# One casting queue for all loads, statistics batched by two pairs, and the last store moved: a small post-norm kernel

## The chip, the cores and the metric

The kernel runs on one core of a Trainium2 chip. The metric is the device time of one execution in microseconds (us). Each comparison runs both kernels in rounds on the same chip. A run counts as slow here when it lies over 1.5% above the fastest of the same kernel, for one core has no second die to be compared with.

Profiles name the engines PE (TensorE; PEld is its loading of weights), ACT (ScalarE), DVE (VectorE), POOL (GpSimd) and SP (SyncE, which here only issues transfers); a q at the end is the engine's instruction queue. SBUF is the memory that the engines work in, PSUM the one that TensorE writes to. A transfer is in flight from its issue until it lands, that is until its last part has arrived.

## The reference

```python
# x: (4, 256, 256), w_block: (256, 256), gamma: (256,), all float32
h = np.maximum(x @ w_block, 0.0)
y = x + h
mu = y.mean(-1, keepdims=True)
sigma = np.sqrt(y.var(-1, keepdims=True) + 1e-6)
return ((y - mu) / sigma * gamma).astype(np.float32)
```

## The kernel before

The 1024 rows are eight tiles of 128 rows, worked in four pairs ("waves", here x0 to x3). For a pair: transpose on TensorE, copy to SBUF on ACT, multiply by the weights on TensorE, relu on ACT, add x and take statistics on DVE; then, two pairs later in the program, square root on ACT, reciprocal and scale on DVE, normalise (one tile on DVE, one on ACT), multiply by gamma, store. The first pair and the weights come over SP's queue in fp32, the rest over GpSimd's, which casts to bf16 on the way.

```python
psum_t16 = tc.tile_pool(name="psum_t16", bufs=2, space=PSUM)
ident16, ident32 = ...                              # made on GpSimd
nc.sync.dma_start(x32_head, x_v[:, 0:WAVE, :])      # first pair, fp32, SP
nc.sync.dma_start(w32, w_block.rearrange("(c p) n -> p c n", p=P))
for wv in range(1, n_waves):                        # casting DMAs, GpSimd
    nc.gpsimd.dma_start(x16_rest[:, lo:lo+WAVE, :], x_v[:, wv*WAVE:(wv+1)*WAVE, :])
nc.gpsimd.dma_start(gamma_bc, gamma[None, :].to_broadcast((P, D)))
for c in range(KC):
    nc.vector.tensor_copy(w_sb[:, c], w32[:, c])
nc.scalar.activation(warm, warm, AF.Square)
# ... phase_a(w): transposes, copy xT, products psH, relu y_w, add x ...
for j in range(WAVE):
    nc.vector.bn_stats(bn6[:, j], y_w[:, j])
    nc.vector.bn_aggr(mv[:, j], bn6[:, j])
# ... phase_b(w) ...
nc.scalar.activation(sig, mv[:, :, 1], AF.Sqrt, bias=eps_sb)
nc.vector.reciprocal(rstd, sig)
nc.vector.scalar_tensor_tensor(out=nmr, in0=mv[:, :, 0], scalar=-1.0, ...)
# ... two normalisations into o1, then the multiply by gamma ...
if last:  # fp32, SP
    nc.vector.tensor_mul(of32_last, o1, gamma...); nc.sync.dma_start(dst, of32_last)
else:     # bf16, cast by the store
    nc.vector.tensor_mul(of16_all[...], o1, gamma...); nc.gpsimd.dma_start(dst, of16_all[...])
```

The order in which each engine runs its instructions is not the order of this text: the framework schedules them when the kernel is built.

## Time and profile before

| | |
|---|---|
| time, median of 6 runs | 24.76 us (24.53 to 25.16) |
| span of the profiled run | 23.0 us |
| first transpose starts / first relu starts | 4.54 / 7.37 us |
| last relu ends | 14.51 us |
| last multiply ends / last store lands | 19.05 / 22.1 us |

A timeline line gives start, duration (both us), engine, source line, operation, written and read tiles, shapes, count; in brackets stands how long the engine had been idle and what released it. These are two groups of products of the same shape and number, from the timeline of the kernel before:

```profile
6.30 1.04 PE L113 MATMUL psH<-w_sb,xT 128*128 128x256 bf16 x4 [0.68 <-ACT xT L108]
...
13.26 0.61 PE L113 MATMUL psH<-w_sb,xT 128*128 128x256 bf16 x4 [2.46 <-ACT xT L108]
```

The first four products take 1.04 us, the last four 0.61: TensorE runs slowly until late in the kernel. And this is the first of GpSimd's work after the start-up, in the place that the prediction gives to the first load:

```profile
0.74 0.20 POOL masks.py:197 MEMSET ident_82<- 128x128 bf16 x1 [0.29 <-POOLq L204]
```

### The profile page before, as it was taken

What the parts mean: (1) busy time and instruction counts of PE and PEld (TensorE: products, weight loads), DVE (VectorE), ACT (ScalarE), POOL (GpSimd) and SP (SyncE); (2) the same over time, 40 slices, a digit from 0 to 9 for tenths busy, and PEclk for the clock granted to TensorE, in tenths of its full rate; (3) what the DMA queues carried; (4) which work ended last, traced back from release to release, by engine and by line L of the source; (5) the groups of instructions that cost most, each with busy time, mean ns of one, the idle gap of its engine ahead of it and who ended that gap; (6) DMA issues with size and microseconds to landing.
All of it is one profiled execution on the core that took longest, in us unless ns stands there. A gap on an engine that the chain in (4) does not pass through costs nothing.

```text
span 23.0 us, 195 instructions
## 1 busy us (share of the span) xinstructions
PE 5.9 (26%) x32; PEld 4.0 (17%) x32; DVE 9.5 (42%) x40; ACT 10.2 (44%) x19; POOL 4.9 (21%) x15
## 2 busy tenths in 40 slices
PE   0000000197099949998000091000000000000000
PEld 0000000190078726763000050000000000000000
DVE  0100000016000099829970794699999891000000
ACT  0698000001801995376999937940696900000000
POOL 3699998000000000000000000005301762000000
PEclk9999999999999999999999997555555555555555
DMA  0003569999992000000000000000087029997000
GB/s 0 0 0 136 152 203 301 244 162 123 194 156 36 4 0 0 0 0 0 0 0 0 0 0 0 0 0 0 0 264 193 0 86 371 303 357 246 7 0 0
DMA packets 1568, 2.03 MB, mean 88 GB/s; under 512 B 160, under 2 KB 928, under 8 KB 1568
## 3 DMA queue, kind: packets, MB, share of 16 engines
q0 software_dynamic: 1008, 1.25, 25.9%
q1 hardware_dynamic: 560, 0.79, 10.6%
HBM read 1.44 MB, written 1.05 MB: 108 GB/s over the span
## 4 chain that ended last, share of the span: by engine, by line
ACT 21%; PE 21%; DMA 16%; DVE 12%; issue 5%; POOLq 2%; POOL 2%
DMA x_head<-in_x_dram 16%; PE psH L113 16%; ACT y_w L122 8%; ACT xT L108 7%; ACT L140 6%; PE psT L105 5%; DVE of_all L176 3%; DVE bn_201 L133 3%; POOLq L215 2%; POOL out_dram L181 2%; DVE nmr L144 2%; DVE rstd L142 1%; ACT sig L140 1%; DVE o_224 L151 1%; DVE o_213 L151 1%
## 5 line engine op out<-in xcount | busy, mean ns | idle before, releaser
L181 POOL DMA_DIRECT2D out_dram<-of_all x3 | 1.6, 536 | 13.6 <-DVE of_all L176 12.2
L113 PE MATMUL psH<-w_sb,xT 128*128 128x256 bf16 x16 | 3.6, 382 | 3.5 <-ACT xT L108 3.5
L122 ACT ACTIVATE y_w<-psH 128x512 bf16<-128x512 f32 x4 | 2.4, 597 | 2.6 <-PE psH L113 2.6
L113 PEld LDWEIGHTS <-xT 128*128 128x128 bf16 x16 | 1.7, 128 | 4.8 <-ACT xT L108 4.4
L105 PE MATMUL psT<-ident_87,x_head 128*128 128x128 f32 x4 | 1.1, 428 | 4.5 <-DMA x_head<-in_x_dram 4.5
L79 DVE CAST w_sb<-w_94 128x256 bf16<-128x256 f32 x2 | 0.5, 290 | 4.2 <-DMA w_94<-in_w_block_dram 4.2
L108 ACT CAST xT<-psT 128x512 bf16<-128x512 f32 x1 | 0.6, 585 | 3.4 <-PE psT L105 3.4
L105 PE MATMUL psT<-ident_82,x_rest 128*128 128x128 bf16 x12 | 1.9, 313 | 0.0
L70 POOL DMA_DIRECT2D x_rest<-in_x_dram x3 | 1.7, 587 | 0.0
L124 DVE TENSOR_TENSOR y_w<-y_w,x_head 128x512 bf16<-128x512 bf16 x1 | 0.7, 693 | 2.4 <-ACT y_w L122 2.4
L126 DVE TENSOR_TENSOR y_w<-y_w,x_rest 128x512 bf16<-128x512 bf16 x3 | 1.2, 415 | 1.0 <-ACT y_w L122 1.0
L108 ACT COPY xT<-psT 128x512 bf16<-128x512 bf16 x3 | 1.6, 584 | 0.0
L85 ACT ACT_TABLE_LOAD x1 | 1.3, 1283 | 0.7 <-PEq L204 0.7
L105 PEld LDWEIGHTS <-x_rest 128*128 128x128 bf16 x12 | 1.5, 151 | 0.3
L105 PEld LDWEIGHTS psT<-ident_87,x_head 128*128 128x128 f32 x4 | 0.7, 217 | 4.5 <-issue 4.5
L140 ACT ACT_TABLE_LOAD x1 | 1.3, 1283 | 0.0
L140 ACT ACTIVATE sig<-mv,eps_sb 128x2 f32<-128x2 f32 x4 | 1.2, 288 | 0.0
L160 ACT ACTIVATE o_213<-y_w,nmr,rstd 128x256 bf16<-128x256 bf16 x1 | 0.6, 600 | 1.1 <-DVE nmr L144 1.1
L142 DVE RECIPROCAL rstd<-sig 128x2 f32<-128x2 f32 x4 | 0.6, 160 | 0.9 <-ACT sig L140 0.9
L133 DVE BATCH_NORM_STATS2 bn_127<-y_w 128x6 f32<-128x256 bf16 x2 | 0.8, 418 | 0.0
L133 DVE BATCH_NORM_STATS2 bn_148<-y_w 128x6 f32<-128x256 bf16 x2 | 0.8, 418 | 0.0
L133 DVE BATCH_NORM_STATS2 bn_201<-y_w 128x6 f32<-128x256 bf16 x2 | 0.7, 414 | 0.0
(29 smaller groups left out, 9.8 us busy)
## 6 DMA issues: line engine op xcount, KB each, us to landing
out_dram<-of_all POOLq DMA_DIRECT2D x3, 256.0 KB, 2.8
x_rest<-in_x_dram POOLq DMA_DIRECT2D x3, 128.0 KB, 4.7
x_head<-in_x_dram SPq DMA_DIRECT2D x1, 256.0 KB, 3.7
w_94<-in_w_block_dram SPq DMA_DIRECT2D x1, 256.0 KB, 3.9
out_dram<-of_last SPq DMA_DIRECT2D x1, 256.0 KB, 3.0
gamma_bc<-in_gamma_dram POOLq DMA_DIRECT2D x1, 64.0 KB, 4.7
```

Of the source, the lines that this page charges most:

```text
L70: nc.gpsimd.dma_start(x16_rest[:, lo : lo + WAVE, :], x_v[:, wv * WAVE : (wv + 1) * WAVE, :])
L85: nc.scalar.activation(warm, warm, AF.Square)
L105: nc.tensor.transpose(psT[:, j, c, :], x_of(w, j)[:, ts(c, P)], idt)
L108: nc.scalar.copy(xT, psT)
L113: nc.tensor.matmul(psH[:, j, :], lhsT=xT[:, j, c, :], rhs=w_sb[:, c, :], start=(c == 0), stop=(c == KC - 1),)
L122: nc.scalar.activation(y_w, psH, AF.Relu)
L124: nc.vector.tensor_add(y_w, y_w, x32_head)
L126: nc.vector.tensor_add(y_w, y_w, x16_rest[:, (w - 1) * WAVE : w * WAVE, :])
L133: nc.vector.bn_stats(bn6[:, j], y_w[:, j])
L140: nc.scalar.activation(sig, mv[:, :, 1], AF.Sqrt, bias=eps_sb)
L142: nc.vector.reciprocal(rstd, sig)
L181: nc.gpsimd.dma_start(dst, of16_all[:, lo : lo + WAVE, :])
```

## The change

The intent was to drop the weight casts and the fp32 transposes, to keep SP out, and to halve the number of small statistics operations. The diffs in this document are shortened: dots, and lines in words, stand for code left out.

```diff
-    stats = ...bufs=n_waves + 2        psum_t16 = ...bufs=2
+    stats = ...bufs=4                  psum_t16 = ...bufs=3
+    w_sb = const.tile([P, KC, D], BF16)
+    nc.gpsimd.dma_start(w_sb, w_block.rearrange("(c p) n -> p c n", p=P))
+    x16_all = xin.tile([P, n_tiles, D], BF16)
+    nc.gpsimd.dma_start(x16_all[:, 0:WAVE, :], x_v[:, 0:WAVE, :])
     ident16 = ...
-    ident32, x32_head and w32 on SP, x16_rest
+    for wv in range(1, n_waves):
+        nc.gpsimd.dma_start(x16_all[:, lo:lo+WAVE, :], x_v[:, lo:lo+WAVE, :])
-    for c in range(KC): nc.vector.tensor_copy(w_sb[:, c], w32[:, c])
...
-            nc.vector.bn_aggr(mv[:, j], bn6[:, j])
+            nc.vector.bn_aggr(mv_all[:, w * WAVE + j], bn6[:, j])
-    sqrt, reciprocal, nmr per pair
+    def run_chain(w):                 # once for two pairs
+        nc.scalar.activation(sig_all[:, sl], mv_all[:, sl, 1], AF.Sqrt, bias=eps_sb)
+        nc.vector.reciprocal(rstd_all[:, sl], sig_all[:, sl])
+        nc.vector.scalar_tensor_tensor(out=nmr_all[:, sl], ...)
...
-        if last: fp32 multiply, nc.sync.dma_start(dst, of32_last)
+        nc.gpsimd.dma_start(out_v[...], of16_all[...])     # every pair
```

More of the change, by code (lines that the diff above doesn't have):

```diff
@@ L41 @@
     NORM_V = _env("PNR_NORM_V", 1)
+    LAST_Q = os.environ.get("PNR_LAST_Q", "g")
     x_v = x.rearrange("b s d -> (b s) d").rearrange("(p j) d -> p j d", j=n_tiles)
@@ L50 @@
     opool = ctx.enter_context(tc.tile_pool(name="opool", bufs=1))
-    stats = ctx.enter_context(tc.tile_pool(name="stats", bufs=n_waves + 2))
-    psum_t16 = ctx.enter_context(tc.tile_pool(name="psum_t16", bufs=2, space=bass.MemoryType.PSUM))
+    stats = ctx.enter_context(tc.tile_pool(name="stats", bufs=4))
+    psum_t16 = ctx.enter_context(tc.tile_pool(name="psum_t16", bufs=3, space=bass.MemoryType.PSUM))
     psum_t32 = ctx.enter_context(tc.tile_pool(name="psum_t32", bufs=1, space=bass.MemoryType.PSUM))
     psum_h = ctx.enter_context(tc.tile_pool(name="psum_h", bufs=3, space=bass.MemoryType.PSUM))
+    w_sb = const.tile([P, KC, D], BF16)
+    nc.gpsimd.dma_start(w_sb, w_block.rearrange("(c p) n -> p c n", p=P))
+    x16_all = xin.tile([P, n_tiles, D], BF16)
+    x32_last = None
+    nc.gpsimd.dma_start(x16_all[:, 0:WAVE, :], x_v[:, 0:WAVE, :])
     ident16 = const.tile([P, P], BF16)
     make_identity(nc, ident16)
-    ident32 = const.tile([P, P], FP32)
-    make_identity(nc, ident32)
-    x32_head = xin.tile([P, WAVE, D], FP32)
-    nc.sync.dma_start(x32_head, x_v[:, 0:WAVE, :])
-    w32 = const.tile([P, KC, D], FP32)
-    nc.sync.dma_start(w32, w_block.rearrange("(c p) n -> p c n", p=P))
-    x16_rest = xin.tile([P, n_tiles - WAVE, D], BF16)
-    for wv in range(1, n_waves):
-        lo = (wv - 1) * WAVE
-        nc.gpsimd.dma_start(
-            x16_rest[:, lo : lo + WAVE, :], x_v[:, wv * WAVE : (wv + 1) * WAVE, :]
-        )
+    for wv in range(1, n_waves):
+        lo = wv * WAVE
+        if wv == n_waves - 1 and LAST_Q == "s":
+            x32_last = xin.tile([P, WAVE, D], FP32)
+            nc.sync.dma_start(x32_last, x_v[:, lo : lo + WAVE, :])
+        else:
+            nc.gpsimd.dma_start(x16_all[:, lo : lo + WAVE, :], x_v[:, lo : lo + WAVE, :])
+    ident32 = None
+    if LAST_Q == "s":
+        ident32 = const.tile([P, P], FP32)
+        make_identity(nc, ident32)
     gamma_bc = const.tile([P, D], BF16)
     nc.gpsimd.dma_start(gamma_bc, gamma[None, :].to_broadcast((P, D)))
-    w_sb = const.tile([P, KC, D], BF16)
-    for c in range(KC):
-        nc.vector.tensor_copy(w_sb[:, c], w32[:, c])
     eps_sb = const.tile([P, 1], FP32)
@@ L85, with wave_x @@
     nc.scalar.activation(warm, warm, AF.Square)
-    of16_all = opool.tile([P, n_tiles - WAVE, D], BF16)
-    of32_last = opool.tile([P, WAVE, D], FP32)
-    def x_of(w, j):
-        if w == 0:
-            return x32_head[:, j, :]
-        return x16_rest[:, (w - 1) * WAVE + j, :]
+    of16_all = opool.tile([P, n_tiles, D], BF16)
+    mv_all = stats.tile([P, n_tiles, 2], FP32, tag="mv_all", bufs=1)
+    rstd_all = stats.tile([P, n_tiles], FP32, tag="rstd_all", bufs=1)
+    nmr_all = stats.tile([P, n_tiles], FP32, tag="nmr_all", bufs=1)
+    sig_all = stats.tile([P, n_tiles], FP32, tag="sig_all", bufs=1)
+    chains_done = set()
+    def wave_x(w):
+        if w == n_waves - 1 and x32_last is not None:
+            return x32_last
+        return x16_all[:, w * WAVE : (w + 1) * WAVE, :]
     def phase_a(w):
-        is32 = w == 0
+        xw = wave_x(w)
+        is32 = xw.dtype == FP32
         if is32:
@@ L104, in phase_a @@
             for c in range(KC):
-                nc.tensor.transpose(psT[:, j, c, :], x_of(w, j)[:, ts(c, P)], idt)
+                nc.tensor.transpose(psT[:, j, c, :], xw[:, j, ts(c, P)], idt)
         xT = xtp.tile([P, WAVE, KC, P], BF16, tag="xT")
@@ L122, in phase_a, with phase_b @@
         nc.scalar.activation(y_w, psH, AF.Relu)
-        if is32:
-            nc.vector.tensor_add(y_w, y_w, x32_head)
-        else:
-            nc.vector.tensor_add(
-                y_w, y_w, x16_rest[:, (w - 1) * WAVE : w * WAVE, :]
-            )
+        nc.vector.tensor_add(y_w, y_w, xw)
         bn6 = stats.tile([P, WAVE, 6], FP32, tag="bn6")
-        mv = stats.tile([P, WAVE, 2], FP32, tag="mv")
         for j in range(WAVE):
             nc.vector.bn_stats(bn6[:, j], y_w[:, j])
-            nc.vector.bn_aggr(mv[:, j], bn6[:, j])
-        return y_w, mv
-    def phase_b(w, y_w, mv):
-        last = w == n_waves - 1
-        sig = stats.tile([P, WAVE], FP32, tag="sig")
-        nc.scalar.activation(sig, mv[:, :, 1], AF.Sqrt, bias=eps_sb)
-        rstd = stats.tile([P, WAVE], FP32, tag="rstd")
-        nc.vector.reciprocal(rstd, sig)
-        nmr = stats.tile([P, WAVE], FP32, tag="nmr")
+            nc.vector.bn_aggr(mv_all[:, w * WAVE + j], bn6[:, j])
+        return (y_w,)
+    def run_chain(w):
+        g = w // 2
+        if g in chains_done:
+            return
+        chains_done.add(g)
+        lo = g * 2 * WAVE
+        hi = min(lo + 2 * WAVE, n_tiles)
+        sl = slice(lo, hi)
+        nc.scalar.activation(sig_all[:, sl], mv_all[:, sl, 1], AF.Sqrt, bias=eps_sb)
+        nc.vector.reciprocal(rstd_all[:, sl], sig_all[:, sl])
         nc.vector.scalar_tensor_tensor(
-            out=nmr, in0=mv[:, :, 0], scalar=-1.0, op0=ALU.mult, in1=rstd, op1=ALU.mult
-        )
+            out=nmr_all[:, sl], in0=mv_all[:, sl, 0], scalar=-1.0, op0=ALU.mult,
+            in1=rstd_all[:, sl], op1=ALU.mult,
+        )
+    def phase_b(w, y_w):
+        run_chain(w)
+        t0 = w * WAVE
         o1 = stats.tile([P, WAVE, D], BF16, tag="o1")
         for j in range(WAVE):
+            t = t0 + j
             if j < NORM_V:
@@ L153, in phase_b @@
                     in0=y_w[:, j],
-                    scalar1=mv[:, j, 0:1],
-                    scalar2=rstd[:, j : j + 1],
+                    scalar1=mv_all[:, t, 0:1],
+                    scalar2=rstd_all[:, t : t + 1],
                     op0=ALU.subtract,
@@ L163, in phase_b @@
                     func=AF.Identity,
-                    bias=nmr[:, j : j + 1],
-                    scale=rstd[:, j : j + 1],
-                )
-        dst = out_v[:, w * WAVE : (w + 1) * WAVE, :]
-        if last:
-            nc.vector.tensor_mul(
-                of32_last, o1, gamma_bc[:, None, :].to_broadcast((P, WAVE, D))
-            )
-            nc.sync.dma_start(dst, of32_last)
-        else:
-            lo = w * WAVE
-            nc.vector.tensor_mul(
-                of16_all[:, lo : lo + WAVE, :],
-                o1,
-                gamma_bc[:, None, :].to_broadcast((P, WAVE, D)),
-            )
-            nc.gpsimd.dma_start(dst, of16_all[:, lo : lo + WAVE, :])
+                    bias=nmr_all[:, t : t + 1],
+                    scale=rstd_all[:, t : t + 1],
+                )
+        nc.vector.tensor_mul(
+            of16_all[:, t0 : t0 + WAVE, :],
+            o1,
+            gamma_bc[:, None, :].to_broadcast((P, WAVE, D)),
+        )
+        nc.gpsimd.dma_start(
+            out_v[:, t0 : t0 + WAVE, :], of16_all[:, t0 : t0 + WAVE, :]
+        )
     pend = []
```

## The prediction

> **What bounds the kernel now.** I read the page's chain of waits first (what ended last), then the timeline of all engines, then the list of waits and the forty-slice table of engine use. The chain, from the page of the kernel before:
>
> ```profile
> ## 4 chain that ended last, share of the span: by engine, by line
> ACT 21%; PE 21%; DMA 16%; DVE 12%; issue 5%; POOLq 2%; POOL 2%
> ```
>
> No engine carries it alone: it is latency, one step after another. The busiest engine of all, ACT, is used 44% of the 23.0 us span (10.2 us), DVE 42% (9.5 us). So what counts is the length of a path with three stretches. The first, from the timeline (start us, duration us, engine, line):
>
> ```profile
> 0.75 0.37 SPq L62 DMA_DIRECT2D x_head<-in_x_dram  x1
> 1.17 0.42 SPq L65 DMA_DIRECT2D w_94<-in_w_block_dram  x1
> 1.64 1.74 POOL L70 DMA_DIRECT2D x_rest<-in_x_dram  x3
> ...
> 4.54 1.09 PE L105 MATMUL psT<-ident_87,x_head 128*128 128x128 f32 x4 [4.54 <-DMA x_head<-in_x_dram]
> 5.06 0.50 DVE L79 CAST w_sb<-w_94 128x256 bf16<-128x256 f32 x2 [4.15 <-DMA w_94<-in_w_block_dram]
> 5.66 0.58 ACT L108 CAST xT<-psT 128x512 bf16<-128x512 f32 x1 [3.42 <-PE psT L105]
> ```
>
> **Stretch 1, start to 5.66:** the first x pair is issued at 0.75 and lands 3.7 us later (the page's part 6), at about 4.4; four fp32 transposes take 1.09 us. The weights, issued at 1.17, land at 1.17 + 3.9 = 5.07 and their casts end at 5.56, while the first product starts at 6.30: the weights are not what it waits for.
>
> **Stretch 2, 5.66 to 14.5:** PE and ACT hand four pairs to each other, and a table load stands in the middle, ahead of the last pair's copy:
>
> ```profile
> 10.53 0.60 ACT L122 ACTIVATE y_w<-psH 128x512 bf16<-128x512 f32 x1 [0.36 <-PE psH L113]
> ...
> 11.15 1.28 ACT L140 ACT_TABLE_LOAD   x1
> ...
> 12.44 0.29 ACT L140 ACTIVATE sig<-mv,eps_sb 128x2 f32<-128x2 f32 x1
> 12.64 0.57 ACT L108 COPY xT<-psT 128x512 bf16<-128x512 bf16 x1
> ...
> 13.91 0.60 ACT L122 ACTIVATE y_w<-psH 128x512 bf16<-128x512 f32 x1 [0.51 <-PE psH L113]
> ```
>
> **Stretch 3, 14.5 to 22.1:** from 14.54 to 19.05 DVE is nearly without a gap, so there its work is the bound; then the last store, and 0.9 us of ending (22.1 to 23.0):
>
> ```profile
> 17.87 0.42 DVE L176 TENSOR_TENSOR of_all<-o_224,gamma_bc 128x512 bf16<-128x512 bf16 x1
> 18.36 0.69 DVE L170 TENSOR_TENSOR of_last<-o_235,gamma_bc 128x512 f32<-128x512 bf16 x1
> 18.58 0.53 POOL L181 DMA_DIRECT2D out_dram<-of_all  x1 [0.33 <-DVE of_all L176]
> 19.08 0.35 SPq L173 DMA_DIRECT2D out_dram<-of_last  x1
> ```
>
> The printed times are 24.76 against a profiled span of 23.0; I take the 1.76 between as constant, so a microsecond of span is a microsecond of time.
>
> **What the Trainium skill says.** (1) "DMA: Bandwidth & Descriptors", section "SWDGE vs HWDGE vs iDMA": a cast in a DMA can only be issued from GpSimd. So the change must put every load on one queue, behind one issuer. The trace agrees in form: the only casting transfers are POOL's, each taking POOL 0.54 to 0.67 us. (2) The same page, "Latency and other measured facts", gives first bytes about 0.6 us after issue from SP and about 1 us from GpSimd. The trace is slower for SP: issue at 0.75, and DMA activity begins in the slice that starts at 1.73. For GpSimd it has 15.75 to the slice starting at 16.68, about 0.9 to 1.1 us; so here the two differ little. (3) "ScalarE: Activation LUTs", "What ACT_TABLE_LOAD costs": 1283 ns for any set, the trace's 1283 exactly. The change leaves both loads in. (4) "VectorE: DVE Perf Modes", section on the trn2 errata: small operations pay a fixed cost per instruction, so fewer are cheaper than smaller ones. The trace agrees: a reciprocal of two elements takes 160 ns, and a 128x256 normalisation only 312 to 340.
>
> **The change part by part.**
>
> *Loads.* SP's two go; POOL issues w, x0, then the identity, x1, x2, x3, gamma. POOL is free at 0.74, where it now begins the identities. At 0.55 to 0.7 us each (w has twice the runs, so I take 0.7) w is issued at 0.74 and x0 at about 1.45. First data of w: +1.1 as for the store, or +1.7, because x_rest, issued at 1.64, seems slow in starting among the SP traffic: 1.85 to 2.45. While the POOL loads alone ran (6.33 to 6.90 in the slices), DMA moved 154 GB/s counted in bf16 bytes:
>
> ```profile
> 1.73:2.30 0.57, 0.00 (x0) 0.00 (x0) 0.00 (x0) 0.51 (x2) 0.57 (x1) 1.00 0.38 139
> 6.33:6.90 0.57, 0.57 (x3) 0.40 (x4) 0.00 (x0) 0.00 (x0) 0.00 (x0) 1.00 1.08 154
> ```
>
> so the 128 KB of a pair need 0.8 us and w, in smaller runs, about 1.0 by estimate. x0 has then all its data at 1.85 to 2.45 + 1.8 = 3.65 to 4.25, and with 0.2 us for the completion 3.85 to 4.45: middle 4.1, against 4.4 now. The early slices show why a later issuer need not lose: x0 and w from SP alone moved only 139 and 148 GB/s in fp32 bytes, so x0 did not have the DMA engines' full rate. Gain 0.3.
>
> *bf16 first pair.* Four fp32 transposes (1.09 us) become four bf16: eight take 1.06 us in the same trace, so four take about 0.6 including the first one's latency of 0.3. Gain 0.5, on the path. The copy from PSUM stays (585 against 580 ns). The add of the first pair drops from 693 to 425 ns on DVE and the weight casts (2 x 290 ns) go; both lie where DVE waits for ACT and are worth nothing. Sum of stretch 1: about **0.8 us**, relu0 at 6.57 in place of 7.37. Stretch 2 I carry over unchanged: its products, evictions and table load are the same, a third PSUM buffer removes no wait that the list of waits shows, and the later x pairs land early enough either way.
>
> *Batched statistics.* Four square roots, reciprocals and nmr operations become two each. ACT saves 2 x 0.29 us; DVE saves 2 x 0.16 + 2 x 0.14 = 0.6 us. But pair 2 now waits for pair 3's statistics. After the last relu (14.5 on the old clock) the path is: add 0.42, two bn_stats 0.74, aggregate 0.25, square root 0.29, reciprocal 0.17, nmr 0.16, two ACT normalisations 0.60 + 0.55, last multiply 0.42, hops about 0.15: 3.75, so 18.25. DVE's own work in that window: the same add, stats and aggregate (1.46), reciprocal and nmr 0.33, two normalisations 0.65, two multiplies 0.84, plus what is left of pairs 0 and 1 (up to 2 x 0.42 + 0.32): 3.3 to 4.45, so 17.8 to 18.95. Path and work overlap imperfectly; I take 18.45. The bf16 last multiply (0.42 for 0.69) is in that. Gain over 19.05: **0.6 us**.
>
> *Last store.* It moves from SP to POOL. SP issued 0.03 us after the multiply and landed in 3.0: 3.03. POOL issues 0.29 us after (18.29 to 18.58 for pair 2) and lands in 2.8: 3.09. But both last stores now queue on one issuer: pair 3's can start no sooner than 0.55 after pair 2's, and its data wait behind some 0.9 us of it. I add 0.35: loss **0.4 us**.
>
> Sum: 0.8 + 0.6 - 0.4 = 1.0 us; 24.76 - 1.0 = about 23.7.
>
> **The rivals.**
>
> *A: the loads come later.* If GpSimd's first transfer is slow to begin, or two queued transfers serialise, x0 lands at 5.0 or later, not 4.1. For it: x_rest took 4.3 to 4.9 us from issue to landing, against 3.7 for SP; at that rate x0, issued at 1.45, lands at 5.75. Against: those landings fell in slices where the DMA engines were full (share 1.00 from 3.45 on) with SP's traffic, which is gone. It would turn stretch 1's gain of 0.8 into a loss of up to 0.8: 24.5 to 25.3.
>
> *B: batching makes a bubble.* ACT and DVE both sit idle round the square root of pairs 2 and 3, and four stores bunch at the end. For it: pair 2's statistics are finished by 13.79, and its square root runs at 14.89 before pair 3's are there. Against: DVE is full from 14.54 to 19.05, so what pair 2 could do earlier waits on DVE anyway. With a bubble the 0.6 becomes 0: about 24.3.
>
> *C: stretch 2 shrinks too.* With x1 landed early, its transposes can go into the PE wait during the first copy (0.68 us idle ahead of the first product), and if the square root now waits for pair 1, the last copy may be ordered ahead of the table load, taking out part of PE's 2.46 us wait. That would be worth 0.3 to 1.0 more: 22.7 to 23.4. I can't tell the order in advance.
>
> **Range and chances.** 23.7 is the sum above. A alone gives the top, half of C the bottom: 22.9 to 24.5. Faster by over 2% means under 24.26, that is a gain above 0.5; it fails if A costs the whole of stretch 1, or B comes with half of A. I give 0.78 to faster, 0.17 to within 2%, 0.05 to slower.
>
> **What would show it.** The first transpose at 4.0 to 4.5 and four bf16 transposes within 0.7 us (stretch 1); relu0 near 6.6; two square roots, the second just after pair 3's aggregate; a last multiply of 0.42 us ending near 17.65; the last store issued 0.3 us after that or later, landing some 3.1 to 3.4 after issue, near 21.1. Wrong if the first transpose starts after 5, if DVE or ACT shows a wait over 0.5 us at the second square root that nothing fills, or if the last landing trails the multiply by over 4 us.

## The result

The changed kernel took **25.91 us** in the median of 10 runs (25.11 to 26.59), the kernel before 24.87 us (20 runs). The ratio of the fast runs is **1.0291** (95% interval 1.0227 to 1.0355): 2.9% slower, where 23.7 us was predicted. A ratio is the mean time of one kernel's fast runs over that of the other's of the same rounds, so not quite the ratio of the medians. The fast runs of the changed kernel, the profiled one among them, average 25.28 us (25.11 to 25.45); seven of its ten timed runs lie at 25.8 to 26.6.

From the timeline of the changed kernel:

```profile
1.26 0.82 POOL L58 DMA_DIRECT2D w_sb<-in_w_block_dram  x1 [0.82 <-POOLq L207]
...
2.09 0.56 POOL L62 DMA_DIRECT2D x_all<-in_x_dram  x1
...
6.43 1.30 PE L112 MATMUL psT<-ident_86,x_all 128*128 128x128 bf16 x8 [6.43 <-DMA x_all<-in_x_dram]
...
7.08 1.28 ACT L115 COPY xT<-psT 128x512 bf16<-128x512 bf16 x2 [4.84 <-PE psT L112]
...
7.71 1.89 PE L120 MATMUL psH<-w_sb,xT 128*128 128x256 bf16 x8
8.79 0.60 ACT L129 ACTIVATE y_w<-psH 128x512 bf16<-128x512 f32 x1 [0.43 <-PE psH L120]
...
12.52 1.28 ACT L146 ACT_TABLE_LOAD   x1
...
13.82 0.30 ACT L146 ACTIVATE sig_all<-mv_all,eps_sb 128x4 f32<-128x4 f32 x1
14.15 0.18 DVE L147 RECIPROCAL rstd_all<-sig_all 128x4 f32<-128x4 f32 x1 [0.81 <-ACT sig_all L146]
...
14.31 0.39 DVE L130 TENSOR_TENSOR y_w<-y_w,x_all 128x512 bf16<-128x512 bf16 x1
...
18.38 0.42 DVE L177 TENSOR_TENSOR of_all<-o_207,gamma_bc 128x512 bf16<-128x512 bf16 x1
18.61 1.05 POOL L182 DMA_DIRECT2D out_dram<-of_all  x2 [0.84 <-DVE of_all L177]
```

Read it against the lines of the prediction. The first transpose starts at 6.43 instead of 4.54, the first relu at 8.79 instead of 7.37. Yet the last relu (end 12.5) is 2.0 us *earlier* than before (14.51), because the table load now comes after it and not ahead of the last pair's copy. Then DVE idles 0.81 us behind that load, with the last pair's add (14.31) queued behind the reciprocal although its relu was done at 12.5. The last multiply ends at 18.80, 0.25 us earlier than before, and the last store lands at 22.2, 0.1 later. The span ends 1.17 us after that instead of 0.86.

The page of the changed kernel, in forty slices of 0.585 us, shows where the early time went:

```profile
DMA  0000199939999800000000000000029873993000
GB/s 0 0 0 0 16 133 140 72 51 151 170 193 186 111 12 0 0 0 0 0 0 0 0 0 0 0 0 0 0 74 375 252 196 112 403 319 63 0 0 0
```

Nothing moves until the fifth slice (2.34 us), and in the eighth and ninth (4.1 to 5.3 us) only 72 and 51 GB/s do, although the DMA engines show as busy in one of them. In the trace's list of packets thirteen of 1024 bytes that start between 3.84 and 5.02 us last 0.5 to 1.3 us each, where the median of that size is 0.1: packets, by their time those of the first pair, stand.

### The profile page after: what moved, and what is told of

The parts are those of the page before. It is cut to its first block, busy times and chain, and to the rows that moved or that the text cites. A ratio compares the mean times of both kernels' runs of the same rounds, so it can differ in the third digit from the quotient of the medians.

```text
span 23.4 us, 185 instructions
## 1 busy us (share of the span) xinstructions
PE 4.8 (21%) x32; PEld 3.1 (13%) x32; DVE 8.3 (35%) x34; ACT 10.0 (43%) x17; POOL 6.3 (27%) x16
## 3 DMA queue, kind: packets, MB, share of 16 engines
HBM read 1.44 MB, written 1.05 MB: 107 GB/s over the span
## 4 chain that ended last, share of the span: by engine, by line
DMA 18%; ACT 16%; PE 13%; POOL 11%; issue 11%; DVE 9%; POOLq 2%; DVEq 0%
DMA x_all<-in_x_dram 18%; PE psH L120 11%; ACT y_w L129 7%; POOL out_dram L182 7%; ACT L146 5%; POOL w_sb L58 4%; DVE bn_189 L134 3%; PE psT L112 3%; POOLq L218 2%; ACT xT L115 2%; DVE of_all L177 1%; DVE y_w L130 1%; ACT sig_all L146 1%; DVE o_169 L160 1%; DVE mv_all L135 1%
## 5 line engine op out<-in xcount | busy, mean ns | idle before, releaser
L130 DVE TENSOR_TENSOR y_w<-y_w,x_all 128x512 bf16<-128x512 bf16 x4 | 1.6, 408 | 8.5 <-ACT y_w L129 8.5
L115 ACT COPY xT<-psT 128x512 bf16<-128x512 bf16 x4 | 2.2, 589 | 5.0 <-PE psT L112 4.8
L112 PE MATMUL psT<-ident_86,x_all 128*128 128x128 bf16 x16 | 2.0, 287 | 6.5 <-DMA x_all<-in_x_dram 6.4
L120 PE MATMUL psH<-w_sb,xT 128*128 128x256 bf16 x16 | 3.0, 347 | 0.5 <-ACT xT L115 0.5
L112 PEld LDWEIGHTS <-x_all 128*128 128x128 bf16 x16 | 1.5, 133 | 6.9 <-DMA x_all<-in_x_dram 6.8
L73 POOL DMA_DIRECT2D x_all<-in_x_dram x3 | 1.6, 554 | 0.0
L87 ACT ACT_TABLE_LOAD x1 | 1.3, 1283 | 0.7 <-PEq L207 0.7
L146 ACT ACT_TABLE_LOAD x1 | 1.3, 1283 | 0.0
L58 POOL DMA_DIRECT2D w_sb<-in_w_block_dram x1 | 0.8, 825 | 0.8 <-POOLq L207 0.8
L169 ACT ACTIVATE o_202<-y_w,nmr_all,rstd_all 128x256 bf16<-128x256 bf16 x1 | 0.6, 599 | 0.7 <-DVE nmr_all L148 0.7
L169 ACT ACTIVATE o_169<-y_w,nmr_all,rstd_all 128x256 bf16<-128x256 bf16 x1 | 0.6, 599 | 0.7 <-DVE nmr_all L148 0.7
L134 DVE BATCH_NORM_STATS2 bn_121<-y_w 128x6 f32<-128x256 bf16 x2 | 0.8, 418 | 0.0
L134 DVE BATCH_NORM_STATS2 bn_161<-y_w 128x6 f32<-128x256 bf16 x2 | 0.8, 418 | 0.0
L134 DVE BATCH_NORM_STATS2 bn_141<-y_w 128x6 f32<-128x256 bf16 x2 | 0.8, 418 | 0.0
L134 DVE BATCH_NORM_STATS2 bn_189<-y_w 128x6 f32<-128x256 bf16 x2 | 0.7, 412 | 0.0
L146 ACT ACTIVATE sig_all<-mv_all,eps_sb 128x4 f32<-128x4 f32 x2 | 0.6, 298 | 0.3 <-DVE mv_all L135 0.3
L169 ACT ACTIVATE o_207<-y_w,nmr_all,rstd_all 128x256 bf16<-128x256 bf16 x1 | 0.6, 585 | 0.0
L169 ACT ACTIVATE o_194<-y_w,nmr_all,rstd_all 128x256 bf16<-128x256 bf16 x1 | 0.6, 584 | 0.0
```

The source lines that it names most:

```text
L58: nc.gpsimd.dma_start(w_sb, w_block.rearrange("(c p) n -> p c n", p=P))
L73: nc.gpsimd.dma_start(x16_all[:, lo : lo + WAVE, :], x_v[:, lo : lo + WAVE, :])
L112: nc.tensor.transpose(psT[:, j, c, :], xw[:, j, ts(c, P)], idt)
L115: nc.scalar.copy(xT, psT)
L120: nc.tensor.matmul(psH[:, j, :], lhsT=xT[:, j, c, :], rhs=w_sb[:, c, :], start=(c == 0), stop=(c == KC - 1),)
L130: nc.vector.tensor_add(y_w, y_w, xw)
```

## The experiments

**Theory at the start:** the late first pair, and to a lesser part the last store, cost more than the batching gains. **Rival:** the batching makes a bubble, the loads are hidden. Eighteen further runs were made, one of them of the changed kernel itself, all with correct results.

### Each part alone, and the changed kernel again

`loads_only`: the kernel before with all loads as changed (w first, casting), and, since bf16 now has four pairs, three PSUM buffers.

```diff
-    psum_t16 bufs=2; x0 and w on SP in fp32, casts on DVE
+    psum_t16 bufs=3; nc.gpsimd.dma_start(w_sb, ...); nc.gpsimd.dma_start(x16_all[:, 0:WAVE, :], ...)
```

> The kernel before with only the loads changed: weights and all four x pairs by casting GpSimd DMAs, w first, bf16 transposes throughout; statistics per pair and the last store on SP in fp32 as before. Theory 1 (the loads cost): the first x pair lands near 6.4 us instead of 4.4, bf16 transposes give back 0.5, so relu0 starts 1.2 to 1.5 us later than before's 7.37 and the time is 0.4 to 1.0 us above before (25.2 to 25.8). Theory 2 (the batching costs, the loads are hidden): within 0.2 us of before, 24.6 to 25.0.

Measured: fast runs 24.84 to 25.18, mean 24.98; ratio 1.0104 (1.0035 to 1.0173). The pair landed at 6.41 us and relu0 started 1.44 us late, as theory 1 said, but the cost was 0.27 us, between the two theories. What made up the rest was not clear then; `before_3buf` below answers it.

`batch_only`: only `run_chain` and `mv_all` added to the kernel before.

```diff
-    sqrt, reciprocal, nmr for each pair
+    sqrt, reciprocal, nmr once for two pairs
```

> The kernel before with only the statistics batched per two pairs; loads and stores as before. Theory 1: two square roots, reciprocals and nmr instead of four take about 0.5 us out of the last stretch: 24.2 to 24.5. Theory 2 (batching makes a bubble while pair 2 waits for pair 3): 0.2 to 0.6 us slower, 25.0 to 25.4, with DVE or ACT idle over 0.5 us at the second square root.

Measured: one fast run at 24.35, four at 24.74 to 24.86, one at 25.19; no ratio, so inconclusive by itself, but no loss. The profile fell in a slow run and is not used for times.

`store_only`: only the last store changed.

```diff
-            nc.vector.tensor_mul(of32_last, ...); nc.sync.dma_start(dst, of32_last)
+            nc.vector.tensor_mul(of16_all[...], ...); nc.gpsimd.dma_start(dst, of16_all[...])
```

> The kernel before with only the last store changed: bf16 multiply and a casting GpSimd DMA in place of an fp32 multiply and an SP DMA. The multiply takes 0.42 instead of 0.69 us. Theory 1: that 0.27 us is more than lost, since the store queues behind the one before it on GpSimd and lands 0.3 us later than on SP, and GpSimd's closing drain then ends 0.3 us later than SP's wait did: 0.2 to 0.5 us slower. Theory 2: neutral, within 0.1 us.

Measured: fast runs 24.89 to 24.97, ratio 1.008 (1.0047 to 1.0113). So 0.2 us are lost net, although the multiply is 0.27 us shorter: theory 1, at its lower edge.

`after_again`: the changed kernel, no edit.

> The changed kernel itself again, for a second profile and more times. The first profile had packets of the first x pair standing for 0.5 to 1.3 us each between 3.8 and 5.2 us. If that stall belongs to the kernel it recurs with the first x pair landing at 6.2 to 6.6 us; if it is chance, the pair lands near 5.0 us in this profile. Times 25.1 to 26.6 as in the first ten runs.

Measured: 25.23 to 26.25, first pair landed at 6.30 us. The late landing belongs to the kernel.

### The table load

`after_sqrtwarm` and `before_sqrtwarm`: one word in each kernel, nothing reordered on any engine, the second table load gone.

```diff
-    nc.scalar.activation(warm, warm, AF.Square)
+    nc.scalar.activation(warm, warm, AF.Sqrt)
```

> The changed kernel with its warm-up activation a square root instead of a square, so that one table load at the start serves all; every other instruction in the same order. In the changed kernel the table load (12.5 to 13.8 us) now stands between the last relu and the first square root and DVE idles 0.8 us for it. Theory 1a (the batched first square root waits behind that load, which is where the batching's gain went): the first square root starts near 12.5 instead of 13.8, the last multiply ends 0.7 to 1.2 us earlier (about 17.8) and the time falls by 0.5 to 1.1 us, to 24.2 to 24.7 in the fast state. Rival (the stores set the end whatever comes before): under 0.3 us.

> The same one-word change to the kernel before, as the control. There the load stood ahead of the last pair's copy, so it should gain 0.7 to 1.2 us as well (23.6 to 24.1) if the load was on its path too. If the changed kernel gains clearly more than this one, the change had made the load more exposed; if the same, the load was equally on both paths and does not explain the difference between them.

Measured: the changed kernel 24.28 and 24.29 in the fast state (ratio to before 0.9799; 0.9729 to 0.9868), the kernel before 23.39 to 23.71 (ratio 0.9484; 0.9381 to 0.9588). The load was on both paths and worth about 1.0 and 1.2 us. It does not explain the difference between the kernels; theory 1a was right that the load is exposed, wrong that this sets the two apart.

### What the first pair waits for

`after_x0first`: first pair issued ahead of the weights.

```diff
-    nc.gpsimd.dma_start(w_sb, ...)       # w, then x0
+    nc.gpsimd.dma_start(w_sb, ...)       # moved below x0's
```

> The changed kernel with the first x pair issued ahead of the weights. Theory: the weights' issue (0.82 us on GpSimd) and transfer stand ahead of x; then x is issued at 1.26 instead of 2.09 and lands 0.8 us earlier or more, 5.0 to 5.6. If packets of x stand still because the engines are stalled at a fixed time (3.8 to 5.2 us), x lands before that, near 3.9 to 4.4, and the weights land late, 5.5 to 6. If the standing belongs to reading x first, x lands at 5 or later with a spread of over 1 us among its sixteen parts. The time: 0 to 0.5 us faster, since the weights are needed 1.2 us after x only.

Measured: x0 issued at 1.24, landed at 5.12 (3.9 us in flight), its sixteen parts spread over 1.45 us, with five packets of 0.8 to 1.0 us that start at 3.1 to 3.4 us; the time 24.54 in the one fast run (25.07 to 25.48 otherwise). The weights' turn does cost, and the standing packets travel with the pair: they are not tied to a time. Its products started only at 7.18, because TensorE's order in the changed kernel puts the second pair's transposes ahead of the first product, and x1 landed at 6.74.

`after_gate`: later loads held back by one-element GpSimd copies that read x0. It is slower on purpose.

```diff
+            nc.gpsimd.tensor_copy(x16_all[:, lo, 0:1], x16_all[:, 0, 0:1])
             nc.gpsimd.dma_start(x16_all[:, lo : lo + WAVE, :], ...)     # likewise ahead of gamma
```

> The changed kernel with the later loads (x1, x2, x3, gamma) held back until the first x pair has landed, by one-element copies on GpSimd that read it. Later loads come late on purpose; the whole will be slower (26 to 28 us). What counts is when the first x pair lands: if it is the later loads, queued or being issued, that hold it up, it lands by 5.0 us with a spread under 0.7 us; if not, at 6.2 to 6.5 as before.

Measured in one look, 29.45 us. The view of the first pair's tile, for the DMA issued at 2.1 us:

```profile
L62 POOL DMA_DIRECT2D x_all<-in_x_dram x1: 558/558/558, 2.1 to 2.1; - x1
...
DMA to landing us min/median/max: 4.2/4.2/4.2
```

The changed kernel has 4.3 there. The later loads do not hold the pair up.

`after_touch`: an early SP DMA reads one element of x for each partition.

```diff
+    touch = xin.tile([P, 1], FP32)
+    nc.sync.dma_start(touch, x_v[:, 0, 0:1])
```

> The changed kernel with one extra early SP DMA that reads one element of x for each of the 128 partitions into a tile nobody uses. In every kernel so far the first transfer that reads x spreads its sixteen landings over 1.3 to 1.8 us, with packets standing 0.5 to 1.3 us, whether it is the first on its queue or the second and with nothing queued behind it. If that is a cost of reading that memory for the first time, the touch pays it early (0.75 to about 3 us): x0's landings spread under 0.7 us and end by 5.2 to 5.5 instead of 6.3, and the time falls by 0.3 to 0.9. If not, x0 lands at 6.2 to 6.5 as before.

Measured: x0 landed at 5.81, 3.7 us after issue, half a microsecond earlier, still spread over 1.1 us (the spread without it reached 1.9 in `loads_only`, beyond the 1.8 named above). So a first-touch cost is at most a part. x1 landed at 7.90 instead of 7.08 and, by TensorE's order, took the first product with it (8.35 instead of 7.71): 25.89 to 26.13, ratio 1.047. A miss for the time. What makes the packets stand stays **open**.

### TensorE's rate

`after_hotpe`: twelve unused products during the first load; `before_hotpe` (later) the same with eight.

```diff
+    hot = const.tile([P, 512], BF16); nc.vector.memset(hot, 1.0)
+    for _ in range(12):      # 8 in before_hotpe
+        nc.tensor.matmul(ps_hot, lhsT=hot[:, 0:P], rhs=hot, start=True, stop=True)
```

> The changed kernel with twelve unused 128x512 matmuls on TensorE while it waits for the first load (1 to 6 us). In the profiles of the changed kernel the second half of the products took 1.10 us for eight and in runs elsewhere 1.03 for four; its times spread from 25.1 to 26.6. If the spread is TensorE running at half rate for a longer or shorter time, it goes away: all runs within 0.4 us, the eight products near 1.1 us in both halves, the times 24.4 to 24.9. If the spread comes from the loads, it stays over 1 us.

> The kernel before with eight unused 128x512 matmuls on TensorE during its first load: the control to after_hotpe. Its products (1.04 us for four) should take 0.6 each time, three of them on the path. If half rate weighs on both kernels alike it gains 0.6 us or more (24.1 or less), and half rate does not explain the difference between them. If it weighs on the changed kernel alone: 24.5 to 24.8. Its times at a granted clock of 1.0 (25.1 to 25.4) should no longer appear.

From the timeline of `after_hotpe`:

```profile
1.46 5.30 PE L88 MATMUL ps_hot<-hot 128*128 128x512 bf16 x12 [1.46 <-DVE warm L93]
...
8.00 0.60 PE L127 MATMUL psH<-w_sb,xT 128*128 128x256 bf16 x4
...
8.84 0.61 PE L127 MATMUL psH<-w_sb,xT 128*128 128x256 bf16 x4 [0.24 <-ACT xT L122]
...
10.62 1.10 PE L127 MATMUL psH<-w_sb,xT 128*128 128x256 bf16 x8 [0.72 <-ACT xT L122]
```

Every group of four now takes 0.6 us. All six runs lie within 24.57 to 24.99 (ratio to before 0.9976; 0.991 to 1.0041), against 25.11 to 26.59 without: the changed kernel's wide spread was for the most part TensorE's rate. The rest has the loads in it: in this trace x1 landed at 7.72 instead of 7.08, and the first product started at 8.00 instead of 7.71; and the slow run of `after_sqrtwarm` (24.68) has the fast run's rates but x1 at 7.69. The Trainium skill, "TensorE: Matmul & The Clock Gate", Part 1, says that an idle TensorE is held at half rate and is released after some 3.4 us of activity, in a window that runs freely; the halved durations, the trace's clock entries (one at full rate lasts 3.41 us, or twice that) and the chance from run to run agree with it. The control gains as well: fast runs 23.51 to 23.84 (one at 25.04), ratio 0.9576 (0.9519 to 0.9634). So half rate costs the kernel before 1.0 us in its fast state and the changed kernel 0.5. It explains most of the spread, and not the difference: 24.76 against 23.71 is still 1.05 us.

The traces also say what the slow state of the kernel before is. They hold entries of the clock granted to TensorE, and the first full one starts at 10.66 us in the kernel before. In all traces, products ahead of that entry take 0.39 to 0.42 us each and those within it 0.27 to 0.29, but for a few that straddle its start or end; in `before_hotpe` the last three products come after its end and take 0.42 again. Four traces have no entry (`batch_only`, `before_sqrtwarm`, `best3`, `after_gate`); their record says "clock 1.0", and all sixteen products take 0.39 to 0.42. So 1.0 means here that TensorE never got full rate. Of the runs of the kernel before beside these experiments all 29 slow ones (25.08 to 25.52) carry 1.0 and all 30 fast ones 0.78 to 0.816: getting full rate in time, in the trace for the last four products, is worth about 0.5 us. In the changed kernel the two overlap (slow 0.795 to 0.835, fast 0.784 to 0.813).

### The last store, and the batching in its place

`after_spstore`: the last store back on SP in fp32.

```diff
+            of32_last if last else of16_all[...]
+        if last: nc.sync.dma_start(out_v[...], of32_last)
```

> The changed kernel with the last store on SP in fp32 again, loads and batching as changed. The fp32 multiply ends 0.27 us later, but the store leaves 0.03 us after it instead of queueing behind the store before it, and the closing drain of GpSimd ends with the third store. If the end after the last landing (1.2 us against 0.9) is GpSimd's drain: that shrinks to 0.9 and the time falls by 0.2 to 0.4 us against the changed kernel's fast runs, to 24.8 to 25.1. If the stores' bandwidth alone sets the end: no change, 25.1 to 25.4.

Measured: fast runs 24.71 and 25.06, ratio to before 1.0027 (0.9911 to 1.0142), so about 0.4 us better than the changed kernel's 25.28. The end after the last landing (22.05 to the span's 22.9) is back at 0.86 us. The view of the closing line in the kernel before, in the changed kernel and in this one (number, min/median/max ns, first and last start):

```profile
L215 POOLq DRAIN  x3: 34/97/3104, 18.6 to 22.7; - x3
```

```profile
L218 POOLq DRAIN  x3: 39/90/3579, 19.1 to 23.1; - x3
```

```profile
L223 POOLq DRAIN  x3: 34/95/3232, 18.4 to 22.6; - x3
```

The long drain is the first one. It ends at 18.6 + 3.1 = 21.7 in the kernel before and 18.4 + 3.2 = 21.6 here, before SP has seen its own store land; in the changed kernel at 19.1 + 3.6 = 22.7, 0.45 us after the last landing, and the end waits for it.

`after_unbatched`: the statistics per pair again.

```diff
-        g = w // 2
-        lo = g * 2 * WAVE;  hi = min(lo + 2 * WAVE, n_tiles)
+        g = w
+        lo = g * WAVE;      hi = lo + WAVE
```

> The changed kernel with the statistics per pair again (four square roots), so that loads and last store are changed and the batching is not. Loads alone were +0.25 us and the last store alone +0.2 us in the fast state. If the parts add up: 25.1 to 25.2, no faster than the changed kernel's fast runs (25.1 to 25.45), and the batching is worth nothing or a loss here. If the batching pays as it did alone (24.35 against 24.6 to 24.8): 25.4 to 25.6. The order of instructions says that the table load moves ahead of the third and fourth relu and the first store goes out near 15.6 us instead of 16.3.

Measured: fast runs 25.09 to 25.45, mean 25.27; ratio 1.0185 (1.0108 to 1.0261). The batching is worth nothing in the changed kernel, or a loss of up to a quarter of a microsecond by the ratios (1.0291 against 1.0185, intervals overlapping). It puts the first square root behind all four relus and the table load.

### The first pair back on SP, and one buffer

`after_x0sp`: first pair on SP in fp32, both identities made before the GpSimd loads; weights, other pairs, batching and last store as changed.

```diff
+    ident16 and ident32 made first
-    nc.gpsimd.dma_start(x16_all[:, 0:WAVE, :], x_v[:, 0:WAVE, :])
+    x32_first = xin.tile([P, WAVE, D], FP32); nc.sync.dma_start(x32_first, x_v[:, 0:WAVE, :])
```

> The changed kernel with the first x pair on SP in fp32 again and both identities made before the GpSimd loads, as in the kernel before; weights, later pairs, batching and last store as changed. TensorE's order is then that of the kernel before. If the late first pair is the main loss: the first pair lands at 4.4, relu0 starts near 7.4, and the fast runs come to 24.5 to 24.9, a gain of 0.4 to 0.7 us on the changed kernel. If the late load is mostly made up for later, as the loads alone suggested: 25.0 to 25.2, a gain of at most 0.25.

Measured: fast runs 23.22 and 23.40, ratio 0.943 (0.9372 to 0.9487), four others 24.0 to 24.4. Against the changed kernel's 25.28 that is a gain of 2.0 us, far above both expectations. Two of the others, 24.01 and 24.42, never got full rate (clock 1.0), and still lie under every run of the changed kernel (25.11 at least); so at least 0.7 us of the gain is not TensorE's rate. From its timeline (of a slow run; the fast ones have no trace):

```profile
0.74 0.36 SPq L67 DMA_DIRECT2D x_first<-in_x_dram  x1
...
3.98 1.09 PE L113 MATMUL psT<-ident,x_first 128*128 128x128 f32 x4 [3.98 <-DMA x_first<-in_x_dram]
...
5.75 1.04 PE L121 MATMUL psH<-w_sb,xT 128*128 128x256 bf16 x4 [0.68 <-ACT xT L116]
...
6.82 0.60 ACT L130 ACTIVATE y_w<-psH 128x512 bf16<-128x512 f32 x1 [1.13 <-PE psH L121]
...
8.66 2.77 PE L121 MATMUL psH<-w_sb,xT 128*128 128x256 bf16 x12
...
9.76 0.60 ACT L130 ACTIVATE y_w<-psH 128x512 bf16<-128x512 f32 x1 [0.27 <-PE psH L121]
```

Alone on SP the pair lands at 3.85 us, 2.5 us before the changed kernel's and also 0.55 before the old one's, which shared SP with the weights. The first product no longer stands behind the second pair's transposes, either. Up to the first relu the traces part the two: in the changed kernel's fast run the first copy ends at 7.66 and the first product starts at 7.71, so the order cost next to nothing there. The first relu is 1.97 us earlier here, which is the 2.53 of the landing less 0.56, mostly for transposes in fp32. Behind it this slow run has lost the lead: all three later pairs are transposed before the second product group (8.66), and the second relu starts at 9.76, in the changed kernel at 9.64. What the fast runs keep of the lead, and where, no trace shows.

`before_3buf`: one number in the kernel before.

```diff
-    psum_t16 = ...bufs=2
+    psum_t16 = ...bufs=3
```

> The kernel before with three instead of two PSUM buffers for the bf16 transposes, one number changed. All three copies then go ahead of the second and third relu and of the table load; DVE's order is unchanged. If the loads' lateness was hidden by this reordering in loads_only (25.0): the last relu ends near 13.3 instead of 14.5 and the time is 0.5 to 1.3 us below before, 23.4 to 24.2, so that the late loads cost 0.8 to 1.5 us. If the buffer is worth nothing: 24.6 to 24.8, and the late loads cost only 0.25.

Measured: fast runs 23.76 to 24.02, mean 23.93, ratio **0.971** (0.9606 to 0.9815). From its timeline:

```profile
7.83 1.56 ACT L108 COPY xT<-psT 128x512 bf16<-128x512 bf16 x3
...
9.54 1.25 ACT L122 ACTIVATE y_w<-psH 128x512 bf16<-128x512 f32 x2
...
10.80 1.28 ACT L140 ACT_TABLE_LOAD   x1
...
12.30 0.58 ACT L122 ACTIVATE y_w<-psH 128x512 bf16<-128x512 f32 x1
```

Compare the prediction's third block of lines: there the last copy came after the table load, at 12.64. With a third buffer the schedule puts all three copies ahead of it, and the last relu ends at 12.88 instead of 14.51. The buffer removed a wait that the list of waits does not name as one for a buffer (it shows TensorE waiting for the copy, 2.5 us), since it sat in the order of instructions. The same third buffer is in `loads_only`, so there its gain stands against the loads' cost.

### Versions that beat both

`best1` is `batch_only` with the square-root warm-up, `best2` the same with eight unused products, `best3` is `after_x0sp` with the store on SP, the square-root warm-up and six unused products.

> The kernel before with the warm-up square root and the batched statistics; loads and last store as before. before_sqrtwarm is at 23.4 to 23.8. If batching pays without the table load in its way: 22.9 to 23.4. If it makes a bubble and bunches the stores: 23.4 to 23.9.

> The same as best1 with eight unused matmuls keeping TensorE busy during the first load. Four products of 1.04 us become 0.6 each, three or four on the path: 0.6 to 1.5 us under best1, 21.9 to 22.8. If the stores' bandwidth sets the end by then, less: 22.8 to 23.2.

> What the runs point to, taken together: the changed kernel with the first x pair on SP and the identities first, the last store on SP in fp32, the warm-up a square root, and six unused matmuls during the first load. after_x0sp had 23.2 to 23.4; the store gives 0.3, the table load about 0.9, TensorE at full rate 0.5: 21.6 to 22.4 by the sum; 22.0 to 22.8 if the four stores' bandwidth takes over as the bound.

Measured: `best1` 23.14 to 23.27 in the fast state, ratio 0.9389 (0.9354 to 0.9424), 0.36 us under `before_sqrtwarm`'s mean of 23.57. That the batching pays with no table load in its way is not shown by that: the intervals of the two ratios overlap, and runs with a like clock differ little or the other way (at 1.0, 24.04 against 23.71 and 23.84; at 0.83, 23.58 twice against 23.62 and 23.39). `best1`'s fast runs had 0.803 to 0.806, for which `before_sqrtwarm` has no run. `best2` 22.14 and 22.23, ratio **0.8976** (0.8939 to 0.9012), the fastest here, though two of its six runs took 23.9. `best3` 22.56 to 22.86, ratio 0.9209 (0.9076 to 0.9343): at the upper edge of what was expected. In its profile, a slow run at 23.74, six unused products did not bring TensorE to full rate: four products still took 1.03 us.

## Why the prediction was wrong

Two things are to be explained: that the kernel did not gain a microsecond, and that it lost. The loss lies behind the last multiply: in the two profiled runs the changed kernel is 0.25 us ahead there, and then loses 0.35 us until the last landing and 0.30 until the end. With the last store back on SP (`after_spstore`) it cannot be told from the kernel before (1.0027; 0.9911 to 1.0142). That the lead was 0.25 us there, where the prediction had 1.4 (17.65 against 19.05), is the loads' doing and, second, the batching's. Of the prediction's own signs of being wrong the first came (first transpose after 5 us, at 6.43) and the third did not (the landing trails the multiply by 3.4 us, not over 4). Its 24.76 - 1.0 is 23.76, rounded down to 23.7.

The runs make a ladder, each step one part more, by the means of the fast runs:

| kernel | fast mean, us | step, us | ratio to before |
|---|---|---|---|
| before (beside the first four runs) | 24.71 | | 1 |
| + third PSUM buffer (`before_3buf`) | 23.93 | -0.78 | 0.971 |
| + all loads by casting GpSimd DMAs (`loads_only`) | 24.98 | +1.05 | 1.0104 |
| + last store on GpSimd (`after_unbatched`) | 25.27 | +0.29 | 1.0185 |
| + batching (the changed kernel) | 25.28 | +0.01 | 1.0291 |

The means come from different rounds; those of the kernel before lie within 24.70 to 24.82 in the later calls, so by that scatter a step is good to about 0.1 us. The ratios give the last two steps as 0.8% and 1.1%. Two more things lie in the +1.05. TensorE got full rate at 9.81 us in the trace of `before_3buf` and at 12.86, behind its last product, in that of `loads_only`; by the 0.5 us above this may be a good part of it. And the order changes with the loads: in `loads_only` the table load (11.25) stands ahead of the third and fourth relu, in `before_3buf` (10.80) ahead of the fourth alone. No run takes these apart from the late landing. That the late first pair costs much in any case, `after_x0sp` shows: 0.7 us at least whatever TensorE's rate, though its order differs too.

- **The loads are the step that failed**: "x0 has then all its data at 1.85 to 2.45 + 1.8 = 3.65 to 4.25 ... middle 4.1, against 4.4 now. Gain 0.3." It landed at 6.38, and the first relu came at 8.79 where 6.57 was predicted. The 1.98 us by which the landing trails SP's 4.40 split by the profiles into 0.51 of a later first issue (1.26 for GpSimd, 0.75 for SP), 0.83 of waiting for the weights' issue (2.09) and 0.64 more in flight (4.29 against 3.65). The prediction took GpSimd to be free for a DMA at 0.74, where a memset started; a DMA in that place starts at 1.26, and the weights' issue took 0.82 where 0.7 was assumed. And it put the flight at 2.65 us from issue, by adding up transfer times, although the row for x_rest said 4.3 to 4.9. That row was quoted under rival A, and dismissed as SP's traffic; without that traffic it is still 4.1 to 4.4, in the eight runs with w first and no load on SP. **Rival A is what happened**, with a landing even later than its 5.75.
- **The bf16 transposes** were right: four took 0.61 us (predicted 0.6). They could not make up for the landing.
- **"Stretch 2 I carry over unchanged ... a third PSUM buffer removes no wait"** was wrong by 0.78 us in the kernel's favour. It is rival C by another door, and it hid more than two thirds of the ladder's +1.05.
- **The batching**, predicted at 0.6 us, gave nothing here. In the changed kernel the first batch stands behind the table load, with 0.81 us of wait on DVE: rival B in size, but not in place, for B had the bubble at the second square root. There DVE stays busy, and ACT waits 0.75 us (to 17.25) for its next normalisation. Without the table load the changed kernel gains 1.0 us (`after_sqrtwarm`), but so does the kernel before; whether the fewer operations are then worth anything stays open (`best1`).
- **The last store**, predicted at 0.4 us: the landing trails the multiply by 3.4 us, as worked out (3.09 + 0.35). The cost of queueing was right. GpSimd's closing drain, 0.3 us more, was not in the sum.
- **Half rate of TensorE** was in no step. With it lifted the kernels are still 1.05 us apart, but it is most of why the changed kernel's runs range over 1.5 us.

## What to carry to other kernels

Take a transfer's time from issue to landing from the profile's own row for that queue, not from bytes over bandwidth plus a start, and give the transfer on which everything waits a queue of its own. A buffer count can change the order in which a scheduler issues instructions, so compare the order of instructions before arguing that a stretch carries over. A table load that the first warm-up activation could have covered, and a TensorE left idle while the first load flies, cost about 1.2 and 1.0 us in this kernel of 24.7. And look at the recorded clock before two kernels' fast runs are compared: here "fast" meant other shares of the products at full rate in each kernel.

## What the Trainium skill lacked or had wrong

- "DMA: Bandwidth & Descriptors", Latency and other measured facts: it gives about 0.6 us to the first byte from SP and about 1 us from GpSimd. In the traces' lists of packets the first load from SP takes 1.0 us (issue 0.75, first packet 1.75) and the first one from GpSimd 1.5 us (1.26, 2.80). And that first DMA on GpSimd started at 1.26 us where a memset in that place started at 0.74; no page has this delay.
- The same page, Anatomy of one DMA: its fit of 2.0 us plus bytes over 436e3 gives an estimate of 2.6 us for the 262144 bytes of a pair in fp32. The page states the fit for GpSimd's transfers. The stores from there agree roughly (2.7 to 3.1 us in the changed kernel); the first load of x does not (4.2 us in `after_gate`, with only the weights ahead). Why packets of the first pair stand is open.
- "ScalarE: Activation LUTs", What ACT_TABLE_LOAD costs: it adds about 1.4 us of drain to the 1283 ns of a load. Here the load began 0.02 us after the relu before it ended (12.50, then 12.52), the next activation started 0.01 to 0.02 us after the load's end (12.52 + 1.28, then 13.82), and leaving the load out gained 1.2 us in the kernel before.
- No page says that the end of a kernel waits for GpSimd's drain after its last DMA, which ended 0.45 us after the last landing in the changed kernel, with the end of the span 1.17 us after the landing instead of 0.86.
- "TensorE: Matmul & The Clock Gate", Part 1, agrees with the durations (1.04 and 0.61 us for four products). What no page has is how to read the profile's clock row: it shows 9 tenths also ahead of the trace's first clock entry (10.66 us in the kernel before), where four products take 1.04 us, and a recorded mean of 1.0 is that of a run without any entry.
